# A fused spectral filter and gated MLP: more buffers of rounded rows, a shorter fetch ahead of the first blocks, and another place for some small work

## The chip, the cores and the metric

The kernel runs on one core of one Trainium2 chip. The metric is the time of one execution on the device in microseconds (us), as the median of several runs. A profile is one execution with the hardware's profiler on.

## What is computed

```python
def reference(A_x, A_w_r, A_w_i, B_x, B_W_gate, B_W_up, B_W_down):
    x = A_x                                   # (1, 2048, 448)
    xn = layernorm(x)                         # over the 448 columns
    # spectral branch: a filter in the 2D frequency domain
    a = irfft2(rfft2(xn) * (A_w_r + 1j * A_w_i), s=(2048, 448))
    # gated branch, F = 1792
    gate = xn @ B_W_gate
    h = relu(gate) * (xn @ B_W_up)
    return x + a + h @ B_W_down
```

Inputs and output are float32.

## The kernel before

**Tiling.** The 2048 rows (tokens) form 16 blocks of 128 rows; block n2 holds every sixteenth row. Four blocks form a chunk q (blocks q, q + 4, q + 8, q + 12), 512 tokens wide, and the chunks are worked on in the order 0, 2, 1, 3. The 1792 hidden columns form 14 slabs f of 128, and the slabs three groups of 5, 5 and 4. Every product runs in float16 with operands split into a rounded value and the rest of it ("hi" and "lo"), so that one float32 product becomes several passes.

**The rows.** For a block, `ln_stats` and `ln_rstd` (DVE, one square root on ACT) work out the mean and the reciprocal deviation, four blocks together. `ln_xn` (L227) writes the normalised row xn on DVE, `ln_hi` (L235) rounds it into the float16 tile tt on ACT, and POOL copies two pieces of tt (L243, L244); `ln_lo` (L252) writes the rest of the rounding beside it on DVE (L254, L255). Then the tile goes transposed into Tq[q], the right-hand side of the products: for chunk 0 with transposes on PE and copies from PSUM (L267, `ln_ev`), for the other chunks with a transposing DMA on SP's queue (L261). There are two tt buffers, taken in turn, and two xn buffers.

**The weights of gate and up.** Each slab and matrix g is one load wst of 128 x 512 (L175, six buffers). `w_sq` squares it on ACT and sums (L525), POOL adds the sums across partitions (L528, `partition_all_reduce`), `w_scale` makes a power of two out of the sum in four small DVE operations (L537 to L541), and `w_hl` writes the scaled hi on ACT (L548) and lo on DVE (L549) into wt. The last of the four operations of `w_scale` (L541) leaves the slab's inverse scale in eg, which only `wd_scale` reads.

**W_down.** For a group, `wd_max` takes the maxima of its slabs' rows on DVE (L554) and across partitions on POOL (L556). `wd_scale` works out scales from them and from eg of the group's slabs (L563 to L570), and `wd_split` writes hi on ACT and lo on DVE (L575, L576).

**The products.** A unit ("gu", f, q) multiplies slab f by chunk q on PE: 20 products of 512 columns (L589) for gate and up, and half passes of 64 rows (L596), which stand together for two units. `gu_post` makes h: relu on ACT (L621), times up on DVE (L622), hi on ACT (L624), lo on DVE (L625). A unit ("dn", g, n2) multiplies h of a group by W_down for one block (L637, 448 columns), and DVE adds the result to xy (L643). The spectral branch (four-step transforms as products, with butterflies on DVE) is a list `bg` of background work.

**What sets the order.** PE, DVE, ACT and SP follow an order written out for the first stretch: warming products on PE (L830), then blocks 0, 4, 8, 12 of chunk 0 with slabs 0 and 1, in the `with tc.manual_schedule` part. Behind it a scheduler decides. The plan is a list `units` of gu and dn units; `sched(i, fn)` hangs work on unit i (slab f's `w_sq` five units ahead of its first use, `w_scale` four, `w_hl` three; `wd_max` five units back, `wd_scale` and `wd_split` three to one), and `run_bg` gives each unit its share of the background. Work that hangs on a unit is issued after an anchor, the last DVE instruction of an earlier unit (`anchors`, `after(LAG)`). POOL runs in program order of what it is given. In the written part POOL is not in the list of ordered engines.

**What the change touches.** `ln_rstd` (L204), the tt and xn buffers (L218 to L233), `ln_lo`, `ln_ev`, `w_scale` (L530), `gu_post` (L619), the offsets of `wd_max`, `wd_scale` and `wd_split` (L816 to L819), the written order (L834 and on), and `after` (L914).

Of the kernel before, what the change touches and what calls it, by code (L numbers as in the profile page):

```python
# [116 lines left out]
def tile_gfnet_reglu(ctx: ExitStack, tc: tile.TileContext, x, xr, wgu, wd, wf, ident, c_fd, c_fm, c_im, c_id, out):  # L117
# [37 lines left out]
    def ft(shape, dt, name, bufs=1):  # L155
        return fwd_pool.tile(shape, dt, name=name, bufs=bufs)
# [8 lines left out]
    def load_xr(n2):  # L165

        xr_b[n2] = free.pop(0)
        xr_t[n2] = xr_b[n2].rearrange("p g c k -> p (g c k)")[:, 0:D]
        nc.sync.dma_start(xr_t[n2], xrv[:, n2, :])
# [9 lines left out]
    def load_wn(eng=nc.sync):  # L179
        if wq:  # L180
            load_w(*wq.pop(0), eng)
# [10 lines left out]
    mv = {}  # L192
# [8 lines left out]

    rst = {}

    def ln_rstd(q):  # L204
        w = ft([128, 6, 4], F32, "rs", 2)
        vv, r0, t, r, nm, sd = (w[:, i] for i in range(6))
        m = mv[q]
        A.activation(sd, m[:, :, 1], AF.Sqrt, bias=eps)
        V.tensor_scalar(vv, m[:, :, 1], 1e-5, None, op0=OP.add)
        V.reciprocal(r0, sd)  # L210
        V.scalar_tensor_tensor(t, r0, -0.5 * 2048, vv, op0=OP.mult, op1=OP.mult)
        V.tensor_tensor(t, t, r0, op=OP.mult)
        V.scalar_tensor_tensor(r, t, 1.5 * 2048, r0, op0=OP.add, op1=OP.mult)
        V.scalar_tensor_tensor(nm, m[:, :, 0], -1.0, r, op0=OP.mult, op1=OP.mult)
        for j in range(4):
            rst[q, j] = r[:, j:j + 1], nm[:, j:j + 1]

    xn, tt = {}, {}  # L218
    tts = [ft([128, 8, 128], F16, f"tt{i}") for i in range(2)]
    for t in tts:  # L220
        G.memset(t[:, 7, 48:64], 0.0)

    def new_tt(n2):
        tt[n2] = tts[state.setdefault("tn", 0) % 2]
        state["tn"] += 1

    def ln_xn(n2, act=True):  # L227
        xn[n2] = ft([128, D], F32, "xn", 2)
        r, nm = rst[n2 % 4, n2 // 4]
        if act:  # L230
            A.activation(xn[n2], xr_t[n2], AF.Identity, scale=r, bias=nm)
        else:
            V.tensor_scalar(xn[n2], xr_t[n2], r, nm, op0=OP.mult, op1=OP.add)  # L233
# [18 lines left out]
    def ln_lo(n2):  # L252
        x, t = xn[n2], tt[n2].rearrange("p a b -> p (a b)")
        V.tensor_tensor(t[:, 512:896], x[:, 0:384], t[:, 0:384], op=OP.subtract)  # L254
        V.tensor_tensor(t[:, 448:512], x[:, 384:448], t[:, 384:448], op=OP.subtract)  # L255

    tp, last = {}, {}

# [10 lines left out]
    def ln_ev(n2, a0, a1, act):  # L269
        q, j = n2 % 4, n2 // 4  # L270
        o = Tq[q][:, a0:a1, 128 * j:128 * (j + 1)]
        if act:
            A.activation(o, tp[n2][:, a0:a1], AF.Copy)
        else:
            last["V"] = V.tensor_copy(o, tp[n2][:, a0:a1]).ins  # L275

# [233 lines left out]


    wt, wdt, wsc = {}, {}, {}
    SMALL = V
    NR = max(GROUPS)


# [13 lines left out]
    def w_scale(f, gs=(0, 1)):  # L530
        m = state["wm", f]
        g = slice(gs[0], gs[-1] + 1)
        n = len(gs)
        sc = mt([128, 2, 2], F32, "wsc", 4)
        e = eg[:, f, g]
        E = SMALL
        E.tensor_scalar(e.bitcast(U32), m[:, 1, g].bitcast(U32), 1, EXPMASK, op0=OP.logical_shift_right,  # L537
                        op1=OP.bitwise_and)
        E.tensor_scalar(sc[:, 0, 0:n], e, TINY * SQ * 2.0 ** -64, 2.0 ** 50 / SQ, op0=OP.max, op1=OP.mult)
        V.reciprocal(sc[:, 1, 0:n], sc[:, 0, 0:n])  # L540
        E.tensor_scalar(e, e, TINY * SQ * 2.0 ** -64, 2.0 ** 64 / SQ, op0=OP.max, op1=OP.mult)  # L541
        for i, k in enumerate(gs):
            wsc[f, k] = sc[:, 1, i:i + 1]

# [73 lines left out]

    def gu_post(f, q):  # L619
        g1 = mt([128, 512], F32, "g1", 3)  # L620
        A.activation(g1, hps[f, q][:, 0, :], AF.Relu, scale=2.0 ** -22)  # L621
        last["V"] = V.scalar_tensor_tensor(g1, hps[f, q][:, 1, :], 2.0 ** -22, g1, op0=OP.mult, op1=OP.mult).ins  # L622
        h = ht[f, q] = mt([128, 2, 512], F16, "h", NR + 2)
        A.activation(h[:, 0, :], g1, AF.Copy)  # L624
        V.tensor_tensor(h[:, 1, :], g1, h[:, 0, :], op=OP.subtract)  # L625
# [167 lines left out]
    def sched(i, fn, *a):  # L793
        at.setdefault(max(i, -1), []).append((fn, a))
# [4 lines left out]
    def gslot(i, back):  # L799
        n = gpos[i] - back  # L800
        return gus[n] if n >= 0 else -1
# [11 lines left out]
            sched(gus[2 + 5 * c], load_x, q + 4 * j)  # L813
    for g, fs in enumerate(groups):
        s = max(i for i in gus if i < first["dn", g])
        sched(gslot(s, 5), wd_max, fs)  # L816
        sched(gslot(s, 3), wd_scale, g, fs)
        for i, f in enumerate(fs):
            sched(gslot(s, 3 - i // 2), wd_split, f, i)  # L819
        for f in (groups[g + 1] if g + 1 < len(groups) else ()):  # L820
            sched(s, load_wd, f)

# [9 lines left out]
    with tc.manual_schedule(engines={mybir.EngineType.PE, mybir.EngineType.DVE, mybir.EngineType.Activation,  # L832
                                     mybir.EngineType.SP}):
        A.activation(mt([128, 1], F32, "root"), eps, AF.Sqrt)  # L834
        for j in range(4):
            load_xr(4 * j)
        load_wn()
        load_wn()
        nc.sync.dma_start(id_t, ident)
        for _ in range(4):  # L840
            load_wn()
        G.memset(warm, 0.0)
        wps = psum.tile([128, 512], F32, name="dn", bufs=2)
        keep_warm(NWARM)
        for j in range(4):
            ln_stats(0, j)
        w_sq(0, (0,))
        ln_rstd(0)
        w_sq(0, (1,))
        for n2 in (0, 4):  # L850
            new_tt(n2)
        ln_hi(0, True)
        w_scale(0, (0,))
        ln_xn(0, False)
        ln_xn(4, False)
        ln_tp(0, (0, 1, 2))
        keep_warm(2)
        ln_lo(0)
        w_hl(0, 0)
        ln_hi(4)  # L860
        ln_tp(4, (0, 1, 2))
        keep_warm(2)
        ln_ev(0, 0, 3, True)
        ln_ev(4, 0, 3, True)
        ln_lo(4)
        gu_open(0, 0)
        gu_full(0, 0, (0,), half[0], True, False, seq1)
        ln_tp(0, (4, 5, 6, 3, 7))
        ln_tp(4, (4, 5, 6, 3, 7))
        w_scale(0, (1,))  # L870
        ln_ev(0, 3, 8, False)
        ln_ev(4, 3, 8, False)
        gu_full(0, 0, (0,), half[0], False, False, seq2)
        for n2 in (8, 12):
            new_tt(n2)
        ln_xn(12, False)
        w_hl(0, 1)
        ln_xn(8, True)
        ln_hi(8)
        gu_full(0, 0, (1,), half[0], True, False, seq1 + seq2)  # L880
        ln_lo(8)
        w_sq(1, (0,))
        ln_hi(12)
        w_sq(1, (1,))
        free.extend(xr_b.pop(4 * j) for j in range(4))
        ln_lo(12)
        ln_tp(8, (0, 1, 2, 4, 5, 6, 3, 7))
        w_scale(1)
        ln_ev(8, 0, 8, True)
        ln_tp(12, (0, 1, 2, 4, 5, 6, 3, 7))  # L890
        ln_ev(12, 0, 8, False)
        gu_full(0, 0, (0,), half[1], False, False, seq1 + seq2)
        w_hl(1, 0)
        w_hl(1, 1)
        gu_full(0, 0, (1,), half[1], False, False, seq1 + seq2)
        for j in range(4):
            load_xr(CHUNKS[1] + 4 * j)
# [10 lines left out]
    took = lambda u: 4.6 if u[0] == "gu" else 0.57 * len(groups[u[1]])  # L908
    nu = sum(took(u) for u in units[RAMP:]) - BGEND
    rate = nbg / nu  # L910
    anchors = [last["V"]]

    @contextmanager
    def after(i):  # L914
        with tc.issue_after(anchors[max(0, len(anchors) - 1 - i)]):
            yield

    for i, u in enumerate(units):
        is_gu = u[0] == "gu"
        if is_gu:  # L920
            _, g, f, q = u
            run_bg(until=marks["T", q])
            gu_unit(f, q, (mates.get(u) or (0, 0, None, None))[2:])
        else:
            _, g, n2, _ = u
            dn_mm(groups[g], n2)
        with after(LAG):
            for fn, a in at.get(i, []):
                with tc.high_priority(offset=200):
                    fn(*a)  # L930
            for v in units[i + 1:i + 1 + AHEAD]:
                if v[0] == "gu":
                    run_bg(until=marks["T", v[3]])
            run_bg(amount=took(u) * rate if i >= RAMP else 0.0)
        if is_gu:
            with tc.high_priority(offset=400):
                gu_post(f, q)
        else:
            if g == len(groups) - 1 and pos[0] < len(bg):
                run_bg(until=len(bg))  # L940
            with tc.high_priority(offset=400):
                dn_post(g, n2)
            if g == len(groups) - 1:
                store(n2)
        anchors.append(last["V"])
    run_bg(until=len(bg))


# [43 lines left out]
```

## Time and profile before

| | us |
|---|---|
| median of 3 runs | 489.31 (488.51 to 489.43) |
| the profiled execution's own time | 489.91 |
| its span, first to last instruction | 488.0 |
| PE busy in the span | 468.8 |
| DVE busy | 383.7 |
| ACT busy | 171.5 |
| POOL busy | 26.4 |
| mean granted TensorE clock | 0.986 |

In the profile's rows PE is TensorE's products, PEld its weight loads, DVE VectorE, ACT ScalarE, POOL GpSimd, and SPq the queue on which SyncE issues DMAs; L261 is line 261 of the kernel. A row of the timeline gives start, duration, engine, line, operation, output <- input, the number of like instructions, and in brackets the idle time of the engine before it with what ended it. A row of the waits gives who waited for whom, us in total, times, longest. A row of the stretches gives, for a stretch from A to B, its length, then for each engine the busy time with its number of instructions, the granted clock, the share of the DMA engines and GB/s.

### The profile page before, as it was taken

What the parts mean: (1) busy time and instruction counts of PE and PEld (TensorE: products, weight loads), DVE (VectorE), ACT (ScalarE), POOL (GpSimd) and SP (SyncE); (2) the same over time, 40 slices, a digit from 0 to 9 for tenths busy, and PEclk for the clock granted to TensorE, in tenths of its full rate; (3) what the DMA queues carried; (4) which work ended last, traced back from release to release, by engine and by line L of the source; (5) the groups of instructions that cost most, each with busy time, mean ns of one, the idle gap of its engine ahead of it and who ended that gap; (6) DMA issues with size and microseconds to landing.
All of it is one profiled execution on the core that took longest, in us unless ns stands there. A gap on an engine that the chain in (4) does not pass through costs nothing.

```text
span 488.0 us, 7692 instructions
## 1 busy us (share of the span) xinstructions
PE 468.8 (96%) x2896; PEld 245.3 (50%) x2896; DVE 383.7 (79%) x928; ACT 171.5 (35%) x340; POOL 26.4 (5%) x61
## 2 busy tenths in 40 slices
PE   6798599999999999999999999999999999999997
PEld 2543145555545555544444444444465655656653
DVE  5897149759893978999999999999999576776642
ACT  4768124322421764243023122262254234323310
POOL 1304000300200000000000000010000000000000
PEclk9899599999999999999999999999999999999999
DMA  7999400500510345432111102010000100010022
GB/s 258 385 375 251 89 0 18 118 17 4 122 29 0 122 123 174 133 107 91 39 40 43 35 19 59 24 40 1 0 23 24 60 12 21 23 69 32 21 75 95
DMA packets 35294, 38.71 MB, mean 79 GB/s; under 512 B 15302, under 2 KB 31430, under 8 KB 35256
## 3 DMA queue, kind: packets, MB, share of 16 engines
q1 hardware_dynamic: 35256, 38.21, 26.1%
q8 instruction: 23, 0.38, 0.3%
q14 instruction: 15, 0.12, 0.1%
HBM read 31.38 MB, written 3.67 MB: 72 GB/s over the span
## 4 chain that ended last, share of the span: by engine, by line
PE 75%; DVE 8%; DMA 5%; ACT 1%; issue 1%; POOL 0%; SPq 0%; ACTq 0%; DVEq 0%; POOLq 0%
PE gu L589 40%; PE dn L637 23%; PE fx L476 4%; PE fx L504 3%; PE gu L596 3%; DMA wmx<-in_wf 2%; DVE small L399 1%; PE fx L287 1%; DVE wt L549 1%; PE fx L329 1%; DMA T<-tt 1%; DMA fm<-in_c_fm 1%; PE fx L331 1%; PE fx L333 1%; DVE wdm L554 1%
## 5 line engine op out<-in xcount | busy, mean ns | idle before, releaser
L589 PE MATMUL gu<-T,wt 128*128 128x512 f16 (+1 forms) x1140 | 257.5, 379 | 1.7 <-DVE T L275 1.5
L589 PEld LDWEIGHTS <-wt 128*128 128x128 f16 x1140 | 110.1, 98 | 133.6 <-issue 15.0
L637 PE MATMUL dn<-wdt,h 128*128 128x448 f16 x672 | 135.8, 352 | 1.1 <-DVE xy L643 1.0
L637 PEld LDWEIGHTS <-h 128*128 128x128 f16 x672 | 65.5, 98 | 62.3 <-issue 2.4
L621 ACT ACTIVATE g<-gu 128x512 f32<-128x512 f32 x56 | 33.3, 594 | 98.4 <-PE gu L596 59.0
L622 DVE SCALAR_TENSOR_TENSOR g<-gu,g 128x512 f32<-128x512 f32 x56 | 38.4, 685 | 21.1 <-ACT g L621 20.8
L624 ACT ACTIVATE h<-g 128x512 f16<-128x512 f32 x56 | 35.1, 628 | 43.7 <-DVE g L622 43.2
L643 DVE SCALAR_TENSOR_TENSOR xy<-dn,dsc,xy 128x448 f32<-128x448 f32 x48 | 32.5, 680 | 20.5 <-PE dn L637 20.3
L625 DVE TENSOR_TENSOR h<-g,h 128x512 f16<-128x512 f32 x56 | 38.4, 686 | 7.9 <-ACT h L624 7.6
L463 DVE SCALAR_TENSOR_TENSOR vt<-y,fsc,vt 128x456 f16<-128x456 f32 x16 | 11.0, 691 | 18.6 <-ACT vt L457 18.6
L596 PE MATMUL gu<-T,wt 64*128 64x512 f16 x112 | 17.4, 390 | 8.1 <-DMA T<-tt 7.1
L548 ACT ACTIVATE wt<-wst,wsc 128x512 f16<-128x512 f32 x28 | 18.6, 711 | 16.7 <-DVE wsc L540 15.9
L476 PEld LDWEIGHTS <-vt 128*128 128x128 f16 x384 | 22.7, 98 | 3.4
L476 PE MATMUL fx<-im,vt 128*128 128x128 f16 x384 | 23.9, 219 | 0.0
L525 ACT ACTIVATE junk<-wst 128x512 bf16<-128x512 f32 x28 | 17.5, 623 | 17.7 <-DMA wst<-in_wgu 17.5
L457 ACT ACTIVATE vt<-y,fsc 128x456 f16<-128x456 f32 x16 | 10.8, 675 | 27.5 <-PE fx L476 22.5
L549 DVE SCALAR_TENSOR_TENSOR wt<-wst,wsc,wt 128x512 f16<-128x512 f32 x28 | 20.3, 743 | 0.0
L492 ACT ACTIVATE pgh<-pg 114x512 f16<-114x512 f32 x16 | 10.1, 630 | 27.9 <-DVE pg L490 27.9
L528 POOL PARTITION_ALL_REDUCE wm<-wm x16 | 8.7, 544 | 180.2 <-ACT junk L525 180.2
L504 PE MATMUL fx<-idc_t,pgh 114*128 114x112 f16 (+1 forms) x192 | 16.4, 236 | 0.0
L319 ACT ACTIVATE Xh<-X 128x456 f16<-128x456 f32 x16 | 9.1, 576 | 19.2 <-DVE X L317 12.2
L243 POOL COPY tt<-tt 128x48 f16<-128x48 f16 x16 | 10.8, 675 | 83.8 <-ACT tt L242 83.1
(102 smaller groups left out, 457.1 us busy)
## 6 DMA issues: line engine op xcount, KB each, us to landing
wst<-in_wgu SPq DMA_DIRECT2D x28, 256.0 KB, 4.7
wmx<-in_wf SPq DMA_DIRECT2D x16, 228.0 KB, 2.6
wf<-in_wf SPq DMA_DIRECT2D x16, 228.0 KB, 2.4
y<-in_xr SPq DMA_DIRECT2D x16, 224.0 KB, 4.8
xy<-in_x SPq DMA_DIRECT2D x16, 224.0 KB, 4.8
out<-xy SPq DMA_DIRECT2D x16, 224.0 KB, 1.9
wdst<-in_wd SPq DMA_DIRECT2D x14, 224.0 KB, 4.2
fm<-in_c_fm SPq DMA_DIRECT2D x16, 192.0 KB, 2.6
```

What stands on the lines that cost most here:

```text
L476: P.matmul(o, v[:, h, w], m[:, c, :], start=(i == 0), stop=(i == 5), skip_group_check=True)
L504: P.matmul(ps[:, o0:o1], h[:, a, i, :], idc_t[:, b, c0:c0 + o1 - o0], start=(j == 0 and i < 3), stop=True, skip_group_check=True)
L548: A.activation(w[:, 0:4, :], st, AF.Copy, scale=sc)
L549: V.scalar_tensor_tensor(w[:, 4:8, :], st, sc, w[:, 0:4, :], op0=OP.mult, op1=OP.subtract)
L589: last["P"] = P.matmul(hps[f, q][:, g, cs], wt[f, g][:, a, :], Tq[q][:, b, cs], start=(start and i == 0), stop=(stop and i == len(seq) - 1 ...
L596: m = P.matmul(hps[f, q][:, g, 0:512], wt[f, g][rows, 7, :], Tq[q][rows, b, :], start=start, stop=not start).ins
L621: A.activation(g1, hps[f, q][:, 0, :], AF.Relu, scale=2.0 ** -22)
L622: last["V"] = V.scalar_tensor_tensor(g1, hps[f, q][:, 1, :], 2.0 ** -22, g1, op0=OP.mult, op1=OP.mult).ins
L624: A.activation(h[:, 0, :], g1, AF.Copy)
L625: V.tensor_tensor(h[:, 1, :], g1, h[:, 0, :], op=OP.subtract)
L637: last["P"] = P.matmul(ps[:, 0:D], ht[f, q][:, a, js], wdt[f][:, b, :], start=(i == 0), stop=(i == n - 1)).ins
L643: last["V"] = V.scalar_tensor_tensor(xy[:, n2, :], dps[n2][:, 0:D], dsc[:, g:g + 1], xy[:, n2, :], op0=OP.mult, op1=OP.add).ins
```

## The change

Seven things, all in one:

- `ln_rstd` takes the blocks that it is to work on; the first two blocks of chunk 0 get their own call, ahead of the other two.
- Four tt buffers instead of two; xn has no buffers of its own, but takes one of the 17 row buffers (`free`), and `ln_lo` gives it back.
- `w_scale`'s last operation (the one that leaves eg) goes from DVE to POOL.
- In the written order, SP fetches two blocks, a slab, the identity, a slab, and then the other two blocks; the first two blocks are normalised and transposed before the rest; slab 0's second half is squared later.
- `wd_max` comes a unit later (two units for the first group), `wd_split` a unit later, and `wd_scale` a unit later for the first group only.
- ACT has anchors of its own: work that hangs on a unit also follows the last ACT instruction (relu) of that unit.
- The `w_sq` of slab 1 are issued together.

```diff
-    def ln_rstd(q):
-        w = ft([128, 6, 4], F32, "rs", 2)
-        vv, r0, t, r, nm, sd = (w[:, i] for i in range(6))
-        m = mv[q]
+    def ln_rstd(q, js=(0, 1, 2, 3)):
+        n = len(js)
+        w = ft([128, 6, 4], F32, "rs", 3)
+        vv, r0, t, r, nm, sd = (w[:, i, 0:n] for i in range(6))
+        m = mv[q][:, js[0]:js[-1] + 1, :]
...
-    tts = [ft([128, 8, 128], F16, f"tt{i}") for i in range(2)]
+    tts = [ft([128, 8, 128], F16, f"tt{i}") for i in range(4)]
...
-        tt[n2] = tts[state.setdefault("tn", 0) % 2]
+        tt[n2] = tts[state.setdefault("tn", 0) % 4]
...
-        xn[n2] = ft([128, D], F32, "xn", 2)
+        xn_b[n2] = free.pop(0)
+        xn[n2] = xn_b[n2].rearrange("p g c k -> p (g c k)")[:, 0:D]
...
         V.tensor_tensor(t[:, 448:512], x[:, 384:448], t[:, 384:448], op=OP.subtract)
+        free.append(xn_b.pop(n2))
...
-            A.activation(o, tp[n2][:, a0:a1], AF.Copy)
+            last["A"] = A.activation(o, tp[n2][:, a0:a1], AF.Copy).ins
...
-        E = SMALL
-        E.tensor_scalar(e.bitcast(U32), ...
+        V.tensor_scalar(e.bitcast(U32), ...
-        E.tensor_scalar(sc[:, 0, 0:n], ...
+        V.tensor_scalar(sc[:, 0, 0:n], ...
         V.reciprocal(sc[:, 1, 0:n], sc[:, 0, 0:n])
-        E.tensor_scalar(e, e, TINY * SQ * 2.0 ** -64, 2.0 ** 64 / SQ, op0=OP.max, op1=OP.mult)
+        G.tensor_scalar(e, e, TINY * SQ * 2.0 ** -64, 2.0 ** 64 / SQ, op0=OP.max, op1=OP.mult)
...
-        A.activation(g1, hps[f, q][:, 0, :], AF.Relu, scale=2.0 ** -22)
+        last["A"] = A.activation(g1, hps[f, q][:, 0, :], AF.Relu, scale=2.0 ** -22).ins
...
-        sched(gslot(s, 5), wd_max, fs)
-        sched(gslot(s, 3), wd_scale, g, fs)
+        sched(gslot(s, 4 if g else 3), wd_max, fs)
+        sched(gslot(s, 3 if g else 2), wd_scale, g, fs)
         for i, f in enumerate(fs):
-            sched(gslot(s, 3 - i // 2), wd_split, f, i)
+            sched(gslot(s, 2 - i // 2), wd_split, f, i)
...
-        for j in range(4):
-            load_xr(4 * j)
-        load_wn()
+        load_xr(0)
+        load_xr(4)
         load_wn()
         nc.sync.dma_start(id_t, ident)
+        load_wn()
+        load_xr(8)
+        load_xr(12)
...
-        for j in range(4):
-            ln_stats(0, j)
+        ln_stats(0, 0)
+        ln_stats(0, 1)
+        ln_rstd(0, (0, 1))
         w_sq(0, (0,))
-        ln_rstd(0)
-        w_sq(0, (1,))
...
-    anchors = [last["V"]]
+    anchors, act_anchors = [last["V"]], [last["A"]]
...
-        with tc.issue_after(anchors[max(0, len(anchors) - 1 - i)]):
+        k = max(0, len(anchors) - 1 - i)
+        with tc.issue_after(anchors[k]), tc.issue_after(act_anchors[k]):
             yield
...
         anchors.append(last["V"])
+        act_anchors.append(last["A"])
```

More of the change, by code (lines that the diff above doesn't have):

```diff
@@ L214, in ln_rstd @@
         V.scalar_tensor_tensor(nm, m[:, :, 0], -1.0, r, op0=OP.mult, op1=OP.mult)
-        for j in range(4):
-            rst[q, j] = r[:, j:j + 1], nm[:, j:j + 1]
-    xn, tt = {}, {}
-    tts = [ft([128, 8, 128], F16, f"tt{i}") for i in range(2)]
+        for i, j in enumerate(js):
+            rst[q, j] = r[:, i:i + 1], nm[:, i:i + 1]
+    xn, tt, xn_b = {}, {}, {}
+    tts = [ft([128, 8, 128], F16, f"tt{i}") for i in range(4)]
     for t in tts:
@@ L512, in tile_gfnet_reglu @@
     wt, wdt, wsc = {}, {}, {}
-    SMALL = V
     NR = max(GROUPS)
@@ L535, in w_scale @@
         e = eg[:, f, g]
-        E = SMALL
-        E.tensor_scalar(e.bitcast(U32), m[:, 1, g].bitcast(U32), 1, EXPMASK, op0=OP.logical_shift_right,
+        V.tensor_scalar(e.bitcast(U32), m[:, 1, g].bitcast(U32), 1, EXPMASK, op0=OP.logical_shift_right,
                         op1=OP.bitwise_and)
-        E.tensor_scalar(sc[:, 0, 0:n], e, TINY * SQ * 2.0 ** -64, 2.0 ** 50 / SQ, op0=OP.max, op1=OP.mult)
+        V.tensor_scalar(sc[:, 0, 0:n], e, TINY * SQ * 2.0 ** -64, 2.0 ** 50 / SQ, op0=OP.max, op1=OP.mult)
         V.reciprocal(sc[:, 1, 0:n], sc[:, 0, 0:n])
-        E.tensor_scalar(e, e, TINY * SQ * 2.0 ** -64, 2.0 ** 64 / SQ, op0=OP.max, op1=OP.mult)
+        G.tensor_scalar(e, e, TINY * SQ * 2.0 ** -64, 2.0 ** 64 / SQ, op0=OP.max, op1=OP.mult)
         for i, k in enumerate(gs):
@@ L844, in tile_gfnet_reglu @@
         keep_warm(NWARM)
-        for j in range(4):
-            ln_stats(0, j)
+        ln_stats(0, 0)
+        ln_stats(0, 1)
+        ln_rstd(0, (0, 1))
         w_sq(0, (0,))
-        ln_rstd(0)
-        w_sq(0, (1,))
         for n2 in (0, 4):
@@ L852, in tile_gfnet_reglu @@
         ln_hi(0, True)
+        ln_xn(0, False)
         w_scale(0, (0,))
-        ln_xn(0, False)
         ln_xn(4, False)
@@ L857, in tile_gfnet_reglu @@
         keep_warm(2)
+        w_hl(0, 0)
         ln_lo(0)
-        w_hl(0, 0)
         ln_hi(4)
+        ln_ev(0, 0, 3, True)
         ln_tp(4, (0, 1, 2))
         keep_warm(2)
-        ln_ev(0, 0, 3, True)
+        ln_stats(0, 2)
+        ln_lo(4)
         ln_ev(4, 0, 3, True)
-        ln_lo(4)
         gu_open(0, 0)
@@ L869, in tile_gfnet_reglu @@
         ln_tp(4, (4, 5, 6, 3, 7))
+        w_sq(0, (1,))
+        ln_stats(0, 3)
+        ln_rstd(0, (2, 3))
         w_scale(0, (1,))
@@ L881, in tile_gfnet_reglu @@
         ln_lo(8)
-        w_sq(1, (0,))
         ln_hi(12)
-        w_sq(1, (1,))
+        w_sq(1)
         free.extend(xr_b.pop(4 * j) for j in range(4))
```

## The prediction

> **What bounds the kernel now.** I read the page's head first, then PE's waits over the span, then PE, SP, ACT and POOL around the longest wait.
>
> ```profile
> span 488.0 us, 7692 instructions
> PE   468.8 (96%) x2896; PEld 245.3 (50%) x2896; DVE 383.7 (79%) x928; ACT 171.5 (35%) x340; POOL 26.4 (5%) x61
> ```
>
> PE works in 96% of the span; only its idle time and its slow time can be saved. PE's waits (us in total, times, longest):
>
> ```profile
> PE gu L596 <- DMA T<-tt: 7.1, 1, 7.1
> PE fx L267 <- ACT tt L240: 2.5, 1, 2.5
> ```
>
> One wait is large. PE in order of time, then the busy time by stretch (columns: length, PE, weight loads, DVE, ACT, POOL, granted clock, DMA share, GB/s):
>
> ```profile
> 45.75 1.30 PE L637 MATMUL dn<-wdt,h 128*128 128x448 f16 x6
> 54.11 1.03 PE L596 MATMUL gu<-T,wt 64*128 64x512 f16 x4 [7.06 <-DMA T<-tt]
> ```
>
> ```profile
> 24.10:47.05 22.95, 22.81 (x110) 10.11 (x108) 20.05 (x62) 17.83 (x38) 4.81 (x10) 1.00 1.05 315
> 47.05:54.11 7.06, 0.00 (x1) 0.01 (x2) 1.24 (x4) 0.85 (x3) 1.70 (x5) 0.67 0.99 224
> 54.11:62.00 7.89, 7.89 (x26) 2.85 (x27) 1.38 (x2) 1.34 (x3) 0.00 (x0) 0.64 0.01 2
> 62.00:160.00 98.00, 98.00 (x595) 51.37 (x593) 71.16 (x188) 29.51 (x57) 8.25 (x16) 1.00 0.18 40
> 160.00:350.00 190.00, 188.62 (x1001) 90.65 (x1000) 179.27 (x411) 64.33 (x133) 5.79 (x11) 1.00 0.22 67
> 350.00:480.00 130.00, 130.00 (x1046) 78.61 (x1044) 92.38 (x212) 43.19 (x79) 0.00 (x0) 1.00 0.11 37
> ```
>
> From 47.05 to 54.11 PE stands for the transposed chunk 2 (T2), and the next 7.89 us run at a granted 0.64: (1 - 0.64) x 7.89 = 2.8 us more. From 62 on PE loses 1.4 us in all. So the kernel is a start of 54.1 us, up to **T2's first half pass**, and a dense rest: whatever moves T2 moves the end, one for one. Why T2 is late, on SP:
>
> ```profile
> 39.73 5.17 SPq L261 DMA_TRANSPOSE T<-tt  x2
> 45.40 2.31 SPq L185 DMA_DIRECT2D wdst<-in_wd  x5
> 47.88 4.14 SPq L261 DMA_TRANSPOSE T<-tt  x2
> ```
>
> ```profile
> 46.27 0.56 ACT L242 ACTIVATE tt<-xn 128x448 f16<-128x448 f32 x1
> ```
>
> Two transposes are issued from 39.73; the other two stand back until ACT may refill the two tt buffers at 46.27.
>
> **The change, part by part.**
>
> *Four tt buffers, xn in the row buffers.* They remove this.
>
> ```profile
> 39.73 1.34 SPq L261 DMA_TRANSPOSE T<-tt  x1
> ```
>
> Four transposes could follow one another some 1.4 us apart: the third would be issued near 39.73 + 2.8 = 42.5; before, 54.11 came 6.2 after the third's 47.88, so T2 would be ready near 48.8. The idle 7.06 would shrink to 2 to 4 us and the slow clock would mostly go. On SP, loads into a row buffer now also wait until its xn is used up, and slab 4's load stands behind such loads; its slot comes free later than they do (DVE's low part of slab 1), so 0.
>
> *The first two blocks and slabs first.* The first sum of squares needs one slab and no longer follows four blocks on the queue; the second rstd adds six small DVE operations, 6 x 0.16 = 1 us by
>
> ```profile
> L213 DVE SCALAR_TENSOR_TENSOR rs<-rs x4: 155/162/164, 9.8 to 122.8; 128x4 f32<-128x4 f32 x4
> ```
>
> and partly ahead of the first weights. Of the same order as PE's 2.5 us wait: gain or loss within 1.5, I take 0.
>
> *W_down's maxima and splits a unit later.* In PE's new order 14 instead of 24 products of W_down stand ahead of T2's half passes. Ten move behind them: by the row at 45.75, 1.30 / 6 = 0.22 less the fill of the first, so 0.20 each, **+2.0 us** of PE work in the dense part.
>
> *ACT's anchors.* ACT's six squares of slabs 5 to 7 leave the stretch of 42 to 47 us for units 14 to 16, and those of 10 to 12 move later too. ACT is busy 43.19 of 130 and 64.33 of 190 us: cover enough, 0.
>
> *w_scale's fourth operation on POOL.* It looks like the smallest edit and I hold it for the largest. On DVE it was 15 operations of 0.148 us in the median, 2.2 us, one an issue's cost.
>
> ```profile
> L541 DVE TENSOR_SCALAR eg<-eg x15: 133/148/225, 10.6 to 325.6; 128x2 f32<-128x2 f32 x13, 128x1 f32<-128x1 f32 x2
> ```
>
> But the changed program's order on POOL shows what is issued for it:
>
> ```
> L542 ISA
> L542 TensorScalarPtr eg<-eg
> L530 ISA
> L530 ISA wm<-wm
> ```
>
> Ahead of each tensor_scalar that follows a cross-partition reduction, and of each reduction that follows a tensor_scalar, stands an instruction without operands: a switch of POOL's function library. Copies and memsets need none. There are 23 in the changed order; before there is one, ahead of the first reduction. No row shows its price; these are the nearest:
>
> ```profile
> 0.82 0.52 POOL L842 MEMSET warm<- 128x512 f16 x1
> 9.10 0.40 POOL L528 PARTITION_ALL_REDUCE wm<-wm  x1 [7.76 <-ACT junk L525]
> 9.90 0.39 POOL L528 PARTITION_ALL_REDUCE wm<-wm  x1 [0.40 <-ACT junk L525]
> 39.64 0.22 POOL L243 COPY tt<-tt 128x48 f16<-128x48 f16 x1
> 39.81 0.23 POOL L244 COPY tt<-tt 128x64 f16<-128x64 f16 x1
> ```
>
> The one switch of before lies in the idle 7.76 us between the memset's end at 1.34 and 9.10, and nothing waited for it visibly: its price c is between 0 and 7.76 us (a second switch under other DMA traffic might cost more). This row is the only one that contains a switch, so I go by it, and stay a reduction's 0.4 below its end since ACT is named as releaser: **c = 7.4 us**. It is the weakest number here; both ends stay in the rivals.
>
> By the Trainium skill, "GPSIMD Engine Reference", section 2.1 "Instruction dispatch", the first call of a freshly loaded POOL kernel pays about 6 us (it gives 5.95 measured) that no instruction in the profile shows. The trace neither agrees nor disagrees, since 5.95 fits into 7.76; the rule speaks against this edit, and its result is the second rival below.
>
> What queues behind it: DVE runs in order, and its reading of each wm waits for POOL. Before that was free:
>
> ```profile
> 34.13 0.17 DVE L537 TENSOR_SCALAR eg<-wm 128x2 uint32<-128x2 uint32 x1 [0.20 <-POOL wm L528]
> ```
>
> In the changed order POOL's work for the first group is a chain: reduction, switch, tensor_scalar, switch, reduction, and so on, with **11 switches** from the first reduction to the tensor_scalar of slab 4. DVE reads the sums (wm) between: its 86th instruction, the first product for W_down's scales, waits for that last tensor_scalar (Pool's semaphore). Behind it in DVE's queue stand all four xn of T2, and behind POOL's tensor_scalar T2's copies into tt. So T2, which before never depended on the slabs' scales, now hangs on all of them.
>
> The walk. First reduction near 10.0 (9.10 before, and six small operations more ahead). Then 7 reductions x 0.40, 4 pairs of copies x 0.40 (39.64 to 40.04), 6 tensor_scalars: no row has one on POOL, so between nothing and a large multiple of the copy's 0.22; 0.15, its price on DVE, is taken, and 1 us each would add 5: 2.8 + 1.6 + 0.9 = 5.3. With 11 x 7.4 = 81.4, slab 4's tensor_scalar ends at 10.0 + 5.3 + 81.4 = 96.7. Then DVE, by rows of before, start to start:
>
> ```profile
> 37.53 0.74 DVE L549 SCALAR_TENSOR_TENSOR wt<-wst,wsc,wt 128x512 f16<-128x512 f32 x1
> 38.19 0.55 DVE L254 TENSOR_TENSOR tt<-xn,tt 128x384 f16<-128x384 f32 x1
> ...
> 38.92 0.55 DVE L254 TENSOR_TENSOR tt<-xn,tt 128x384 f16<-128x384 f32 x1
> ...
> 39.52 0.68 DVE L622 SCALAR_TENSOR_TENSOR g<-gu,g 128x512 f32<-128x512 f32 x1
> 40.12 0.50 DVE L233 TENSOR_SCALAR xn<-y,rs 128x448 f32<-128x448 f32 x1
> 40.54 0.15 DVE L569 RECIPROCAL wds<-wds 128x1 f32<-128x1 f32 x1
> ...
> 41.98 3.07 DVE L576 SCALAR_TENSOR_TENSOR wdt<-wdst,wds,wdt 128x448 f16<-128x448 f32 x5
> ```
>
> 4 xn x 0.42, 2 wt x 0.66, 2 g x 0.60, 4 low parts of tt x 0.60, 2 of h x 0.60, 5 wdt x 0.61, some 0.7 of small ones: 1.7 + 1.3 + 1.2 + 2.4 + 1.2 + 3.1 + 0.7 = 11.6, and 1.0 for ACT and PE between: 12.6. T2's transposes land at about the same time (last low part near 103, 6.2 from the third's issue to T2, as before). Slab 4's two units on PE stand in that stretch too, at first with a slow clock. T2's half passes start near 96.7 + 12.6 = **109.3** instead of 54.1: +55.2.
>
> *Switches later.* Slabs 5 to 9 again alternate. The place, before:
>
> ```profile
> 168.79 0.60 POOL L528 PARTITION_ALL_REDUCE wm<-wm  x1 [4.61 <-ACT junk L525]
> ```
>
> ```profile
> 160.28 0.15 DVE L541 TENSOR_SCALAR eg<-eg 128x2 f32<-128x2 f32 x1
> 176.37 0.16 DVE L537 TENSOR_SCALAR eg<-wm 128x2 uint32<-128x2 uint32 x1
> ```
>
> ```profile
> 160.00:180.00 20.00, 20.00 (x124) 10.64 (x123) 16.82 (x52) 14.00 (x32) 1.60 (x3) 1.00 0.35 116
> ```
>
> In before's times: slab 6's tensor_scalar can run at 160.4; switch, slab 8's reduction, switch, slab 7's tensor_scalar, switch: 160.4 + 3 x 7.4 + 0.6 = 183.2, and slab 9's reduction ends at 183.6. DVE wants it at 176.37: 7.2 late, of which the 3.2 us that DVE has free in 160 to 180 take some. DVE then works 179.27 of 190 us, so I count the other **+4.0**. The last slab's switch lies beside 325 us and is late by one at most: 0.
>
> **Sum**, against the profiled execution's 489.9 (span 488.0 and 1.9 around it; 0.6 over the median of 489.3): 489.9 + 55.2 + 2.0 + 4.0 - 2.8 (PE is at work ahead of T2, so it keeps its clock) = 548.3, **548 us**.
>
> **The rivals.**
>
> *The switch costs nearly nothing (or both libraries stay loaded after their first call).* Then the other parts do what they say. POOL's chain ends at 15.3 + 11c, and T2 at 27.9 + 11c; this stays under 50 us, where loads (DMA share 1.05 to 47 us) and DVE (20.05 of 22.95) hold T2 anyway, as long as c is below 2.0. T2 near 50: 489.9 - 4.1 + 2.0 - 2.8 = **485**, faster. For it: the row at 9.10 shows no cost; against it: that row has a cover of 7.76 us, so it can't show one. It decides the sign at about c = 2.4, where 27.9 + 11c - 54.1 equals 0.8.
>
> *The switch costs 6 us.* The mechanism is the same, at a smaller price, and by the rows equally possible. T2 at 27.9 + 66 = 93.9: 489.9 + 39.8 + 2.0 + 0 to 2 - 2.8 = **530**. The Trainium skill's 5.95 us (the same page and section) would give this.
>
> *The switch is dearer while loads stream.* DMA stands at 1.05 to 47 us in before; if a switch fetches through the same memory, the first three take 10 or more, or c averages 9. T2 at 126.9: 489.9 + 72.8 + 2.0 + 6 - 2.8 = **568**. For it: 315 GB/s from 24 to 47 us; against it: the stalled chain leaves the slots full and the loads end early.
>
> *The switch costs 3 to 5 us*: 497 to 520.
>
> **How the numbers follow.** Forecast (c of 6.7 to 8) 0.48, near 6 0.22, dearer 0.16, 2.4 to 5 0.07, nearly nothing 0.07. The range takes c from 5 to 9: 518 to 568, rounded outward to 516 to 570; outside it are the last two cases and a few hundredths of the dearer one. A measurement can tell about 0.2% (1 us) from no change. Faster 0.07, within 0.2% 0.01, slower 0.92.
>
> **What would show it.** On POOL, gaps of about c with no instruction between tensor_scalar and reduction, from 10 to 97 us; DVE's reads of wm with idle time put down to POOL; PE idle for most of 20 to 100 us at a lower clock; T2's transposes issued back to back; its half passes near 109; a PE as dense as before from there, a second DVE wait on slab 9. If POOL shows no such gaps, or T2's half passes start before 60, the walk is wrong. If the gaps are there but DVE doesn't stand behind them, the chain is wrong and not the price.

## The result, and the profile after

The changed kernel takes 544.57 us (median of 4 runs, 543.28 to 546.01) against 489.37 us, a ratio of 1.113 with an interval of 1.110 to 1.117. It is slower by 55 us; the forecast was 548.

The head of its page (the profiled execution took 543.28 us):

```profile
span 541.4 us, 7721 instructions
PE 476.5 (88%) x2896; PEld 247.8 (46%) x2896; DVE 383.3 (71%) x919; ACT 170.9 (32%) x341; POOL 29.0 (5%) x77
```

The engines have nearly the same to do as before: POOL's 29.0 us are 2.6 more, and PE's 476.5 are 7.7 more, at a mean granted clock of 0.943 instead of 0.986. PE is busy in 88% of the span instead of 96%. POOL, busy in 5% of the span, sets the time. DVE's two waits for it:

```profile
DVE eg L538 <- POOL wm L530: 58.3, 7, 12.6
...
DVE wds L565 <- POOL eg L542: 7.4, 1, 7.4
```

Five of the first row's seven lie in the start, 50.9 us in all. The longest behind it is for slab 9's sum:

```profile
228.60 0.17 DVE L538 TENSOR_SCALAR eg<-wm 128x2 uint32<-128x2 uint32 x1 [6.02 <-POOL wm L530]
```

POOL in order of time (the brackets hold the idle time ahead of each):

```profile
6.07 0.40 POOL L530 PARTITION_ALL_REDUCE wm<-wm  x1 [4.66 <-ACT junk L527]
...
16.64 0.27 POOL L542 TENSOR_SCALAR eg<-eg 128x1 f32<-128x1 f32 x1 [8.97 <-issue]
...
24.59 0.40 POOL L530 PARTITION_ALL_REDUCE wm<-wm  x1 [7.22 <-issue]
31.64 0.27 POOL L542 TENSOR_SCALAR eg<-eg 128x1 f32<-128x1 f32 x1 [6.65 <-issue]
31.96 0.22 POOL L245 COPY tt<-tt 128x48 f16<-128x48 f16 x1
...
39.45 0.40 POOL L530 PARTITION_ALL_REDUCE wm<-wm  x1 [6.75 <-issue]
46.92 0.26 POOL L542 TENSOR_SCALAR eg<-eg 128x2 f32<-128x2 f32 x1 [7.07 <-issue]
53.17 0.41 POOL L530 PARTITION_ALL_REDUCE wm<-wm  x1 [5.99 <-issue]
...
81.60 0.41 POOL L530 PARTITION_ALL_REDUCE wm<-wm  x1 [6.21 <-issue]
89.77 0.26 POOL L542 TENSOR_SCALAR eg<-eg 128x2 f32<-128x2 f32 x1 [7.76 <-issue]
```

Ahead of each later change of kind POOL stands idle for 6 to 9 us. Most of these gaps end with "issue": the profile shows no other engine that POOL waited for. Where neighbours are of one kind, and ahead of a copy, there is no such gap. The 11 gaps from the first reduction up to slab 4's tensor_scalar add up to 77.1 us, 7.0 each. The view of line 542 does show the switches, as instructions of POOL's sequencer (POOLq) of next to no length, two for each of the 11 switches towards a tensor_scalar. The first pair stands at 7.6, at the start of the gap that ends at 16.64:

```profile
L542 POOLq MODIFY_POOL_CONFIG  x22: 5/83/85, 7.6 to 377.4; - x22
```

PE beside it, and then the busy time by stretch (columns as before):

```profile
26.40 3.15 PE L590 MATMUL gu<-T,wt 128*128 128x256 f16 x14 [8.69 <-DVE T L278]
...
55.58 1.04 PE L597 MATMUL gu<-T,wt 64*128 64x512 f16 x4 [10.39 <-DVE wt L550]
...
93.35 7.40 PE L590 MATMUL gu<-T,wt 128*128 128x512 f16 x20 [12.48 <-DVE g L623]
100.58 2.81 PE L638 MATMUL dn<-wdt,h 128*128 128x448 f16 x14
103.33 0.61 PE L597 MATMUL gu<-T,wt 64*128 64x512 f16 x4
...
232.65 0.85 PE L332 MATMUL fx<-Xh,fm 128*128 128x456 f16 x3 [1.56 <-DMA fm<-in_c_fm]
...
236.72 0.61 PE L597 MATMUL gu<-T,wt 64*128 64x512 f16 x4 [1.75 <-DVE g L623]
...
250.86 4.32 PE L638 MATMUL dn<-wdt,h 128*128 128x448 f16 x22 [2.13 <-DVE xy L644]
```

```profile
24.10:54.11 30.01, 8.65 (x50) 5.99 (x49) 5.16 (x19) 8.16 (x17) 2.48 (x9) 0.61 0.25 86
54.11:103.33 49.22, 28.41 (x103) 10.88 (x104) 24.63 (x67) 15.47 (x30) 5.26 (x14) 0.71 0.38 109
103.33:111.00 7.67, 7.67 (x40) 3.54 (x40) 2.60 (x4) 2.45 (x4) 0.00 (x0) 1.00 0.45 145
```

Most of PE's waits name DVE (wt, g, T), since POOL holds DVE and DVE holds PE. PE runs at a granted 0.61 and 0.71 meanwhile, which costs little, because it waits most of the time. Only the end of this stands right ahead of T2: the 20 products from 93.35 take 7.40 us, and the 20 behind T2's half passes 4.49. But T2's transposes are issued from 94.85, and in the kernel with the operation on DVE (below) 7.96 us lay between that point and T2 (41.27 to 49.23). So T2 would have started near 102.8 all the same, and by this estimate the slow clock costs half a us. T2's half passes start at 103.33 instead of 54.11, with no wait in front of them and at full clock. From there to the end of the span it is 438.1 us, against 433.9 before. So 49.2 of the 53.4 us of longer span lie ahead of T2 and 4.2 behind it.

### The profile page after: what moved, and what is told of

Same layout as the page of the kernel before. It is cut to its first block, busy times and chain, and to the rows that moved or that the text cites. A ratio compares the mean times of both kernels' runs of the same rounds, so it can differ in the third digit from the quotient of the medians.

```text
span 541.4 us, 7721 instructions
## 1 busy us (share of the span) xinstructions
PE 476.5 (88%) x2896; PEld 247.8 (46%) x2896; DVE 383.3 (71%) x919; ACT 170.9 (32%) x341; POOL 29.0 (5%) x77
## 4 chain that ended last, share of the span: by engine, by line
PE 69%; issue 19%; DVE 6%; DMA 2%; POOL 1%; ACT 1%; SPq 1%; POOLq 0%; DVEq 0%
PE gu L590 35%; PE dn L638 20%; PE fx L479 4%; PE fx L507 3%; PE gu L597 2%; PE dn L831 2%; PE fx L290 1%; DMA T<-tt 1%; PE fx L332 1%; DVE wt L550 1%; DMA wmx<-in_wf 1%; DVE small L402 1%; DVE wdm L555 1%; DVE g L623 1%; SPq L264 1%
## 5 line engine op out<-in xcount | busy, mean ns | idle before, releaser
L590 PE MATMUL gu<-T,wt 128*128 128x512 f16 (+1 forms) x1140 | 263.9, 386 | 29.9 <-DVE T L278 16.7
L590 PEld LDWEIGHTS <-wt 128*128 128x128 f16 x1140 | 112.4, 100 | 165.5 <-issue 37.4
L538 DVE TENSOR_SCALAR eg<-wm 128x2 uint32<-128x2 uint32 (+1 forms) x15 | 2.4, 160 | 58.3 <-POOL wm L530 58.3
L597 PEld LDWEIGHTS <-wt 64*128 64x128 f16 x112 | 3.3, 95 | 30.0 <-DVE wt L550 18.0
```

Of the source, the lines that this page charges most:

```text
L590: last["P"] = P.matmul(hps[f, q][:, g, cs], wt[f, g][:, a, :], Tq[q][:, b, cs], start=(start and i == 0), stop=(stop and i == len(seq) - 1 ...
L597: m = P.matmul(hps[f, q][:, g, 0:512], wt[f, g][rows, 7, :], Tq[q][rows, b, :], start=start, stop=not start).ins
```

## The experiments

The theory is that of the prediction: the loss is POOL's switches, at the points where they stand in a chain that DVE waits for in order. Its rivals: other parts of the change cost, the moved operation itself is slow, or a switch disturbs more than those who wait.

**The operation back on DVE, all else as changed.**

```diff
-        G.tensor_scalar(e, e, TINY * SQ * 2.0 ** -64, 2.0 ** 64 / SQ, op0=OP.max, op1=OP.mult)
+        V.tensor_scalar(e, e, TINY * SQ * 2.0 ** -64, 2.0 ** 64 / SQ, op0=OP.max, op1=OP.mult)
```

> The changed kernel with w_scale's fourth operation back on DVE; the six other parts stay. Theory (the switches of POOL's library are the whole loss): one switch is left, POOL shows no gap between tensor_scalar and reduction, T2's half passes start near 50 us and the time is 485 us (482 to 488). Rival 1 (the new order of the start, or DVE's new waits in order, costs by itself): T2 starts after 54 us and the time is over 490. Rival 2 (xn in the row buffers or ACT's anchors cost in the dense part): T2 near 50, but over 1 us more idle time of PE behind it than the 1.4 us of the kernel before, 487 to 492.

Measured: 484.05 us, ratio to the kernel before 0.988 (0.985 to 0.991). T2 on PE:

```profile
49.23 0.61 PE L597 MATMUL gu<-T,wt 64*128 64x512 f16 x4 [0.28 <-DMA T<-tt]
```

One operation of 0.26 us on POOL and its switches make 60 us of difference. The six other parts gain 5 us, as the prediction's first rival had them (485). Both of the rivals written for this run are out, by T2 at 49.23 and a time under 487. The same kernel once more, one execution, to see how well such a time repeats:

> Placeholder for the spread between chips: the changed kernel with the fourth operation on DVE once more, one look. 484 us, within 1.5 us.

Measured: 483.4 us.

**That operation alone, in the kernel before.**

```diff
-        E.tensor_scalar(e, e, TINY * SQ * 2.0 ** -64, 2.0 ** 64 / SQ, op0=OP.max, op1=OP.mult)
+        G.tensor_scalar(e, e, TINY * SQ * 2.0 ** -64, 2.0 ** 64 / SQ, op0=OP.max, op1=OP.mult)
```

> The kernel before with only the fourth operation of w_scale moved to POOL. Its order on POOL has 24 switches, 10 of them between the first reduction and the copies for T2's third block. Theory (price of 5.7 to 9 us each, in a chain that holds DVE): 10 x 7.0 and some 17 to 20 us of other work put T2's half passes near 90 to 105 us, 525 to 545 us in all. Rival (the switches cost only with the new order, since there the copies of the first blocks stand between them): under 500 us. Rival 2 (the operation itself is slow on POOL): its rows last several us, with no gaps ahead of them.

Measured: 539.07 us, ratio 1.101 (1.096 to 1.105). On POOL and on PE:

```profile
20.02 0.27 POOL L541 TENSOR_SCALAR eg<-eg 128x1 f32<-128x1 f32 x1 [10.73 <-issue]
...
21.15 0.21 POOL L541 TENSOR_SCALAR eg<-eg 128x1 f32<-128x1 f32 x1
...
82.24 0.26 POOL L541 TENSOR_SCALAR eg<-eg 128x2 f32<-128x2 f32 x1 [7.45 <-issue]
```

```profile
98.93 1.04 PE L596 MATMUL gu<-T,wt 64*128 64x512 f16 x4 [4.54 <-DMA T<-tt]
```

The loss doesn't need the rest of the change. In this stretch the operation itself takes 0.2 to 0.3 us, and the second of the two that have only copies between them has no such gap.

**One operation for a group: a single switch in the start.** `w_scale` leaves it out, and `wd_scale` does it for all slabs of the group:

```diff
-        G.tensor_scalar(e, e, TINY * SQ * 2.0 ** -64, 2.0 ** 64 / SQ, op0=OP.max, op1=OP.mult)
...
+        eb = eg[:, f0:f0 + n]
+        G.tensor_scalar(eb, eb, TINY * SQ * 2.0 ** -64, 2.0 ** 64 / SQ, op0=OP.max, op1=OP.mult)
         V.tensor_tensor(sc[:, 0, 0:n], eg[:, f0:f0 + n, 0], eg[:, f0:f0 + n, 1], op=OP.mult)
```

> The changed kernel, with the fourth operation on POOL but once for all slabs of a group, ahead of W_down's scales: 7 switches behind the first instead of 22, and a single one in the start, between slab 4's reduction and the group's operation. Theory (time = switches in the chain x 7): that one stands in front of DVE's first product of the scales and of T2's xn behind it, so T2 starts 6 to 9 us later than with the operation on DVE, 55 to 60 us, 490 to 495 us in all. Rival (DVE's order doesn't hold T2; only the slabs' weights being late does): as with the operation on DVE, 485.

Measured: 491.85 us, ratio 1.005 (1.002 to 1.007). POOL, DVE and PE:

```profile
43.51 0.31 POOL L565 TENSOR_SCALAR eg<-eg 128x10 f32<-128x10 f32 x1 [7.76 <-issue]
```

```profile
43.85 0.17 DVE L566 TENSOR_TENSOR wds<-eg 128x5 f32<-128x5 f32 x1 [7.44 <-POOL eg L565]
43.94 1.35 DVE L235 TENSOR_SCALAR y<-y,rs 128x448 f32<-128x448 f32 x3
```

```profile
56.70 0.61 PE L598 MATMUL gu<-T,wt 64*128 64x512 f16 x4 [0.49 <-DMA T<-tt]
```

This is the mechanism in one step. POOL's gap of 7.8 us becomes a wait of 7.4 on DVE; the xn of T2, which needs nothing of it, stands behind; T2 moves from 49.23 to 56.70, by 7.5; the span goes from 481.5 to 488.9, by 7.4. The other six switches of this kernel cost nothing that shows: behind T2 both spans have 432.2 to 432.3 us.

**Only the later switches.**

```diff
-        G.tensor_scalar(e, e, TINY * SQ * 2.0 ** -64, 2.0 ** 64 / SQ, op0=OP.max, op1=OP.mult)
+        E = G if f >= 5 else V
+        E.tensor_scalar(e, e, TINY * SQ * 2.0 ** -64, 2.0 ** 64 / SQ, op0=OP.max, op1=OP.mult)
```

> The changed kernel with the fourth operation on DVE for the five slabs of the first group and on POOL for the nine later ones: 10 switches, all behind the start. Theory (the later switches hold DVE at slab 9 and PE behind it, 5.8 us by comparing the part behind T2 of the changed kernel, 438.1 us, with that of the kernel with the operation on DVE, 432.3): T2's half passes at 49 us, one wait of DVE for POOL of 5 to 7 us near 170 us, 488 to 491.5 us in all. Rival (the 5.8 us came from the late start, not from switches): 483.5 to 485. If each of the 10 switches cost its price: 550.

Measured: 490.39 us, ratio 1.0023 (1.0005 to 1.0041), so 6.3 us more than with no such switch (6.4 in the span). T2's half passes start at 49.48. DVE's one large wait, PE's idle times just behind it, and the stretch in which they lie:

```profile
174.86 0.17 DVE L538 TENSOR_SCALAR eg<-wm 128x2 uint32<-128x2 uint32 x1 [6.37 <-POOL wm L530]
```

```profile
178.75 1.02 PE L332 MATMUL fx<-Xh,fm 128*128 128x456 f16 x3 [1.74 <-DMA fm<-in_c_fm]
...
183.16 1.04 PE L598 MATMUL gu<-T,wt 64*128 64x512 f16 x4 [1.17 <-DVE g L624]
184.13 5.97 PE L591 MATMUL gu<-T,wt 128*128 128x512 f16 x20
```

```profile
180.00:190.00 10.00, 8.84 (x33) 3.20 (x32) 8.66 (x16) 1.94 (x5) 1.18 (x3) 0.66 0.60 202
```

Ten switches, of which those ahead of slab 9 reach the path. About half of the loss is idle time of PE behind that wait: 1.7 and 1.2 us, which the kernel without these switches doesn't have. The other half is the lowered clock: the 28 products from 180.21 to 190.10 last 8.8 us in all, and 6.1 in the kernel with the operation on DVE. The two make 5.6 us; where the rest lies was not followed.

**Switches where nobody waits.** In the kernel before, behind POOL's copies for the last block of chunks 1 and 3, on a scratch tile d:

```diff
+        if n2 in (13, 15):
+            d = mt([128, 2, 2], F32, "dum")
+            G.tensor_copy(d[:, 0], t[:, 7, 0:2])
+            for k in (1, 1, 0, 1) if n2 == 13 else (0, 1, 0):
+                if k:
+                    G.tensor_scalar(d[:, 0], d[:, 0], 0.5, 1.0, op0=OP.max, op1=OP.mult)
+                else:
+                    G.partition_all_reduce(d[:, 0], d[:, 0], 128, bass_isa.ReduceOp.max)
```

> The kernel before with extra work on POOL on a scratch tile at two places where POOL is idle for 30 us: behind the copies for chunk 1 (near 94 us) a small copy, two tensor_scalars, a reduction, a tensor_scalar; behind those for chunk 3 (near 132 us) a small copy, a reduction, a tensor_scalar, a reduction. That is 6 more switches, and nothing that matters is queued behind them before 163 us. Theory (a switch costs only those that wait for POOL): gaps of 6 to 8 us in POOL's rows ahead of each change of kind, no gap between the two tensor_scalars that stand together, time as before within 0.2% (488.3 to 490.3). Rival (a switch disturbs others, by its fetch, by a shared port or by PE's clock): longer by several us, with longer operations on DVE or PE at 95 to 155 us. Under the theory that the price comes from streaming loads, the gaps would be shorter here, 2 us or less, since DMA is nearly idle.

Measured: 489.71 us, ratio 1.000 (0.9985 to 1.0017). POOL:

```profile
92.02 0.18 POOL L247 CAST dum<-tt 128x2 f32<-128x2 f16 x1
99.29 0.56 POOL L250 TENSOR_SCALAR dum<-dum 128x2 f32<-128x2 f32 x2 [7.09 <-issue]
105.59 0.37 POOL L252 PARTITION_ALL_REDUCE dum<-dum  x1 [5.74 <-issue]
113.39 0.26 POOL L250 TENSOR_SCALAR dum<-dum 128x2 f32<-128x2 f32 x1 [7.43 <-issue]
...
136.21 0.57 POOL L252 PARTITION_ALL_REDUCE dum<-dum  x1 [5.91 <-issue]
144.44 0.26 POOL L250 TENSOR_SCALAR dum<-dum 128x2 f32<-128x2 f32 x1 [7.66 <-issue]
150.76 0.37 POOL L252 PARTITION_ALL_REDUCE dum<-dum  x1 [6.06 <-issue]
```

Six switches, 39.9 us of POOL's time, and no loss beyond 0.2%: these switches disturbed nobody who didn't wait for them. The price is there with DMA idle too. In four of the six gaps DMA moved 0 to 3 GB/s, and they took 7.43 and 7.66 us towards a tensor_scalar, 5.74 and 6.06 towards a reduction; beside the first (7.09) and the fourth (5.91) it moved 92 and 119 GB/s. The two longest gaps that end with "issue" in any run lie under the heaviest loads: 8.97 at 372 GB/s in the changed kernel, 10.73 at 382 GB/s in the kernel with the operation alone. Each is also its kernel's first switch towards a tensor_scalar, but here the first such took 7.09. That loads lengthen a switch is not shown beyond this: no run changed the loads alone, and below 340 GB/s the gaps don't follow the rate (towards a reduction 7.22 at 333 GB/s in the one, 8.14 at 133 in the other).

**Where the 5 us of the other parts come from.** First the four tt buffers, and xn in the row buffers, alone in the kernel before:

```diff
-    tts = [ft([128, 8, 128], F16, f"tt{i}") for i in range(2)]
+    tts = [ft([128, 8, 128], F16, f"tt{i}") for i in range(4)]
...
```

> The kernel before with only the four tt buffers and xn in the row buffers. Theory (two tt buffers hold back two of T2's transposes): the four are issued one behind the other, PE's wait of 7.1 us shrinks to 2 to 4 us, the clock holds longer, 482 to 486 us. Rival (T2 is then held by the next thing, ACT's six squares and the loads on SP's queue ahead of the transposes): the wait stays at 5 us or more, 487 to 489.

Measured: 483.94 us, ratio 0.988 (0.985 to 0.991). PE and SP:

```profile
49.77 0.61 PE L598 MATMUL gu<-T,wt 64*128 64x512 f16 x4 [1.17 <-DMA T<-tt]
```

```profile
37.33 6.31 SPq L263 DMA_TRANSPOSE T<-tt  x3
44.17 0.82 SPq L175 DMA_DIRECT2D wst<-in_wgu  x2
45.09 1.24 SPq L263 DMA_TRANSPOSE T<-tt  x1
```

The whole gain. Then the changed kernel, with the operation on DVE, with the start written as before (`load_xr` of four blocks first, one `ln_rstd`, slab 1's `w_sq` apart):

> The changed kernel with the fourth operation on DVE and the written order of the start as in the kernel before; four tt buffers, xn in the row buffers, W_down's later places and ACT's anchors stay. Theory (the four buffers carry the whole gain, the new start none): T2's half passes within 2 us of 49, 483 to 486 us. Rival (the new start is needed for T2 at 49): T2 3 us or more later, 487 or more.

Measured: 484.04 us (482.24 to 486.88), ratio 0.991 (0.988 to 0.994); T2's half passes at 50.94. The new start brings PE's first transposes to 8.18 instead of 10.53, and loses it again on the way to T2. Last, the fourth operation on DVE once for a group (as above, with V for G):

> The changed kernel with the fourth operation on DVE once for all slabs of a group, ahead of W_down's scales, instead of once for each slab: 12 fewer small operations on DVE, no further switch. Theory (DVE has cover for them, 0.08 us each): the same as with one for each slab, 483 to 485 us. Rival (the small operations stand in DVE's queue on the path of the start): 1 us or more faster, under 483.

Measured: 483.95 us, ratio 0.989 (0.987 to 0.990), the same. T2 on PE:

```profile
49.16 0.61 PE L598 MATMUL gu<-T,wt 64*128 64x512 f16 x4 [0.47 <-DMA T<-tt]
```

This kernel differs from the one with a single switch in the start by the engine of this operation alone: T2 at 49.16 against 56.70, the span 481.3 against 488.9. So the medians of four versions stand within 0.1 us of 484, about 1% below the kernel before.

**A try for more that went wrong.** Seven buffers for the slabs' loads, in the changed kernel with the operation on DVE:

```diff
-        wst[f, g] = mt([128, 4, 128], F32, "wst", 6)
+        wst[f, g] = mt([128, 4, 128], F32, "wst", 7)
```

> The changed kernel with the fourth operation on DVE, and seven buffers for the slabs' loads instead of six, so that slab 3's second half is loaded ahead of W_down's rows. A try for a faster version. If PE's wait of 4.1 us for slab 3's weights came from that load: the wait goes, but T2's half passes, which start at 49.2 with PE idle for only 0.3 us ahead of them, stay where SP and DVE put them, near 49, so 483 to 484.5 us. Rival (T2 follows slab 4, and slab 4's loads move up too): T2 at 46 to 48, 481 to 483 us.

Measured: 488.54 us, ratio 1.000 (0.998 to 1.002): neither. SP and PE:

```profile
41.77 6.19 SPq L264 DMA_TRANSPOSE T<-tt  x3
48.05 2.44 SPq L185 DMA_DIRECT2D wdst<-in_wd  x5
50.58 1.25 SPq L264 DMA_TRANSPOSE T<-tt  x1
```

```profile
56.54 1.04 PE L597 MATMUL gu<-T,wt 64*128 64x512 f16 x4 [7.54 <-DMA T<-tt]
```

Slab 3's wait went, as expected, and the planner put the next group's five loads of W_down ahead of T2's fourth transpose. On SP's queue they stand until the old rows are used up, so T2 is as late as in the kernel before. That reading comes from the trace alone; no run moved these loads back.

## Why the prediction was right

- *What bounds the kernel, and that the end moves with T2.* Right: T2 moved by 49.2 us and the span by 53.4; with one switch alone by 7.5 and 7.4.
- *Which edit matters.* Right. The rest had been put at 485 us for a free switch; with the operation on DVE it is 484.05.
- *The number of switches in the chain, 11.* Right, as the gaps show.
- *The price, 7.4, from an idle stretch of 7.76 that it could not exceed.* 7.0 in the mean of the 11: 4.3 us less in the chain. But the row that it was taken from did not show it: in the changed kernel the same first switch lies in the 4.66 us ahead of 6.07, so that one costs no more than this. The value was near because the upper end was chosen, not because that row measured it: that is luck. The bound of 7.76 held with DMA idle (7.76 at most, ahead of slab 4's tensor_scalar at 0 GB/s); under loads it was passed, 8.97 and 10.73 at 372 and 382 GB/s, and 8.14 at 133. The third rival had a dearer switch under loads, but 10 us or more for the first three: in the changed kernel they took 8.97, 7.22 and 6.65.
- *The start of the chain.* Wrong by 3.9 us: 10.0 was taken because six operations stand ahead, but slab 0's load, now third on SP's queue, brings the first sum to 6.07. (In the two kernels with the operation on DVE the new start moves it from 8.59 to 6.24.) That term had been put at 0.
- *POOL's other work and DVE behind it.* 6.8 instead of 5.3, and 13.3 (90.03 to 103.33) instead of 12.6.
- *These four together*: -3.9 + 1.5 - 4.3 + 0.7 = -6.0, T2 at 103.3 instead of 109.3. Two terms were too high by 8.2 together and two too low by 2.2.
- *Behind T2.* Predicted +2.0 + 4.0 - 2.8 = +3.2; measured 438.1 - 433.9 = +4.2. DVE waited 6.0 us for slab 9's sum, where 7.2 was expected; against the kernel with the operation on DVE (432.3) the later switches cost 5.8, not 4.0: the 3.2 us of DVE's free time that had been deducted hardly helped. The two other terms, +2.0 - 2.8, came to 432.3 - 433.9 = -1.6.
- *The 6 us of the Trainium skill* ("GPSIMD Engine Reference", section 2.1 "Instruction dispatch", 5.95 measured). The trace agrees in one direction: 5.74, 5.91 and 6.06 towards the reduction, where nobody waited. Towards tensor_scalar it doesn't: 7.09 to 7.66 in the same run, up to 10.73 under loads. So the second rival's 530 us was too low.

What the prediction could not tell from the profile of before is the price itself. It had one such instruction, whose cost lay under a wait.

## What to carry to other kernels

Count what an edit issues, in the order of the built program, before what it computes: an operation of 0.26 us brought 22 switches, 11 of them in a chain that an in-order engine waited for. On POOL, keep tensor_scalars and cross-partition reductions each together, or off POOL if they can run elsewhere for 0.15 us; the switch was free only where nobody waited for what is queued behind it. And where a start is held by one transfer, look at what stands ahead of it on its queue as well as at its buffers: four buffers gained 5 us, and one more load buffer gave them back.

## What the runs showed that was not expected

The price of a switch has a direction: with DMA under 5 GB/s the gaps that end with "issue" took 6.9 to 7.8 us towards tensor_scalar and 5.7 to 6.2 towards the cross-partition reduction. It was highest under the heaviest loads (8.97 and 10.73 at 372 and 382 GB/s), and yet the program's first one, under loads of 231 GB/s, took no more than 4.66; what sets it stays open. In the kernel with only the later switches the clock fell to 0.50 between 180 and 182 us, behind a wait of PE of 1.7 us, and was back at 1.00 by 188. In the changed kernel it stayed at 1.00 behind 1.56, 1.75 and 2.13; why one and not the other stays open.
